# A decode step's attention and MLP in one kernel: the tile framework's scheduling against one section with semaphores of its own, with TensorE's products in hardware loops

## The chip, the cores and the metric

The kernel runs on one core of a Trainium2 chip. The metric is the device time of one launch in microseconds; a time of a kernel is the median of its runs. Durations inside a kernel come from one profiled execution.

## What is computed

One token x of 1024 values goes through a layer norm, and then through two branches whose results are added to it:

```python
xn = layernorm(x)
return x + A(xn, k_cache, v_cache, wq, wo) + B(xn, w1, w2, w3, w4)

# A: 32 query heads, 4 key/value heads, 65536 cached positions of 128 values
q = xn @ wq                                   # 1024 -> 32 x 128
p = softmax(q . k / sqrt(128))                # each of 4 caches serves 8 heads
A = (p @ v) @ wo                              # 4096 -> 1024

# B: two small networks, gelu in its tanh form
h  = gelu(layernorm(xn) @ w1)                 # 1024 -> 1024
hs = shifted(h) @ w2                          # with one token, all shifts give zero
x1 = xn + hs
B  = x1 + gelu(layernorm(x1) @ w3) @ w4       # 1024 -> 3584 -> 1024
```

All inputs are bf16. The two caches are 67 MB each, and everything that is read makes 170 MB.

## The kernel before

**Slots and items.** Three buffers in SBUF, `slot`, hold 128 partitions x 32768 bf16 (8.39 MB) each. The work is a list of items, and an item is what fills one slot: `wq`, `K(g,r)` and `V(g,r)` (g is one of four cache heads, r one of two halves of 32768 positions), `w3`, `w12` (w1 and w2), `w4`, and three items of `wo` (20 rows; 8; 3 and 1). Here a row of a weight means one of the blocks of 128 x 1024 that the view splits it into. The order is

wq, K(0,0), V(0,0), w3, w12, K(0,1), V(0,1), K(1,0), V(1,0), ... , K(3,1), w4, V(3,1), wo, wo, wo.

An item is computed when its turn in the list comes; ahead of that, the transfers are issued on SP's queue up to two items further on (line 119). A transfer into a slot waits until the item that held the slot before, three places back, has been computed. The tile framework puts the waits in from the tiles that each instruction reads and writes, and keeps each engine's instructions in the order of the program.

**K.** `compute_K` transposes a slot in place on VectorE in four pieces, `cg` (line 337, blocks of 32 x 32 of 4-byte pairs). After each piece TensorE makes 16 products of 128 x 512 (line 340) that add to four banks of PSUM, `sc`. After the fourth, VectorE takes the maximum (L344), two small transposes on TensorE (L346, L353) spread it as `nball`, ScalarE takes the exponential into `work` (L357), and VectorE transposes that (L359).

**V.** `compute_V` makes 64 products with 32 weight columns each into `oacc` (L393), where four column tiles of TensorE work side by side. For r = 0 the result is kept in `ob`; for r = 1 `group_weights` and `group_end` put both halves together and write the heads' output to `oT` (L408 to L423). So a K that follows a V with r = 1 comes on VectorE after that V's `group_end`.

**Rows.** `row_acc` (L161) multiplies one weight column (`oT`, `hT` or `gT`) with one row in four quarters of 256, each in a column tile of its own, and adds to `psB`:

```python
for j in range(4):
    nc.tensor.matmul(psB[32 * j:32 * j + 1, 0:NQ], lhsT=lhsT, rhs=w_row[:, NQ * j:NQ * (j + 1)], ...)
```

All 28 rows of w4, 8 of w2 and 32 of wo go through it, and so does x itself at the start (L201). `rows_product` (L242) makes the products with wq, w3 and w1. At the end VectorE copies `psB` (L435) and SP writes it out (L436).

Of the kernel before, what the change touches and what calls it, by code (L numbers as in the profile page):

```python
# [17 lines left out]
LOOKAHEAD = 2  # L18
WO_PIECES = (20, 8, 3, 1)
# [3 lines left out]
def kernel(  # L23
# [35 lines left out]
    NQ = NOUT // 4  # L59
    SCALE = float(DH) ** -0.5  # L60

    pad = ctx.enter_context(tc.tile_pool(name="pad", bufs=1))
    pad.tile([P, 96], F32, name="pad_t")
    big = ctx.enter_context(tc.tile_pool(name="big", bufs=SLOTS))
    const = ctx.enter_context(tc.tile_pool(name="const", bufs=1))
    small = ctx.enter_context(tc.tile_pool(name="small", bufs=2))
    ppool = ctx.enter_context(tc.tile_pool(name="pp", bufs=1))
    scr_pool = ctx.enter_context(tc.tile_pool(name="scr", bufs=1))
    ps_S = ctx.enter_context(tc.tile_pool(name="psS", bufs=1, space=bass.MemoryType.PSUM))
    ps_O = ctx.enter_context(tc.tile_pool(name="psO", bufs=1, space=bass.MemoryType.PSUM))  # L70
    ps_M = ctx.enter_context(tc.tile_pool(name="psM", bufs=2, space=bass.MemoryType.PSUM))
    ps_B = ctx.enter_context(tc.tile_pool(name="psB", bufs=1, space=bass.MemoryType.PSUM))
# [4 lines left out]
    wo_v = A_wo.rearrange("(m c) n -> m c n", c=OC)  # L77
# [5 lines left out]
    items = [("wq",), ("K", 0, 0), ("V", 0, 0), ("w3",), ("w12",)]  # L83
# [4 lines left out]
    items.insert(len(items) - 1, ("w4",))  # L88
    items += [("wo", 0), ("wo", 1), ("wo", 2)]

    st = {}

    def work():
        return ppool.tile([P, HF * 512], BF16, name="work")[:]

    def issue(item):
        kind = item[0]
        t = big.tile([P, KEYS], BF16, name="slot")
        if kind == "wq":
            loads = [(0, wq_v)]  # L100
        elif kind == "w3":
            loads = [(0, w3_v)]
        elif kind == "w4":
            loads = [(0, w4_v)]
        elif kind == "w12":
            loads = [(0, w1_v), (KEYS // 2, w2_v)]
        elif kind == "wo":
            pieces = [item[1]] if item[1] < 2 else list(range(2, len(WO_PIECES)))
            loads = []
            for q in pieces:  # L110
                c0 = wo_start[q]
                at = (c0 - wo_start[pieces[0]]) * NOUT
                loads.append((at, wo_v[:, c0:c0 + WO_PIECES[q], :].rearrange("p c n -> p (c n)")))
        else:
            cache = A_k_cache if kind == "K" else A_v_cache
            _, g, r = item
            loads = [(0, cache[0, g, r * KEYS:(r + 1) * KEYS, :].rearrange("(p k) d -> p (k d)", p=P))]
        for at, src in loads:
            nc.sync.dma_start(out=t[:, at:at + src.shape[-1]], in_=src)
        st[item] = t  # L120

    x_bf = const.tile([P, DC], BF16, name="x_bf")
    nc.scalar.dma_start(out=x_bf[:], in_=A_x[0, 0, :].rearrange("(p c) -> p c", c=DC))
    wk0 = work()
    qrow = wk0[:, 0:1024].rearrange("p (b n) -> p b n", b=2)
    psel = wk0[:, 1024:1536].rearrange("p (b m) -> p b m", b=4)
    x_q = wk0[:, 1536:1536 + NQ]
    ones_f = wk0[:, 1792:2048].bitcast(F32)
    nc.vector.memset(x_q, 0.0)
    nc.scalar.dma_start(out=x_q[0:P:32, :], in_=A_x[0, 0, :].rearrange("(j n) -> j n", j=4))  # L130

    n_issued = [0]

    def ensure(upto):
        while n_issued[0] <= min(upto, len(items) - 1):
            issue(items[n_issued[0]])
            n_issued[0] += 1

    ensure(LOOKAHEAD)

    ident_bf = const.tile([P, P], BF16, name="ident_bf")
    make_identity(nc, ident_bf[:])
    ident_f = const.tile([P, P], F32, name="ident_f")
    make_identity(nc, ident_f[:])
    eps_t = const.tile([P, 1], F32, name="eps_t")
    nc.gpsimd.memset(eps_t[:], LN_EPS)
    nc.gpsimd.memset(ones_f, 1.0)  # L147
    xpad = const.tile([P, DC, 32], BF16, name="xpad")
    nc.gpsimd.memset(xpad[:], 0.0)
    QS = P + 24  # L150
    qst = []
    for i in range(2):
        q_ = const.tile([P, 4, QS], BF16, name=f"qst{i}")
        nc.gpsimd.memset(q_[:], 0.0)
        qst.append(q_)

    psB = ps_B.tile([P, 512], F32, name="psB")

    def row_acc(lhsT, w_row):
        for j in range(4):  # L160
            nc.tensor.matmul(psB[32 * j:32 * j + 1, 0:NQ], lhsT=lhsT, rhs=w_row[:, NQ * j:NQ * (j + 1)],  # L161
                             start=False, stop=False, tile_position=(0, 32 * j),
                             skip_group_check=True)

    xT = const.tile([P, DC], F32, name="xT")
    nc.vector.tensor_copy(out=xT[:], in_=x_bf[:])  # L166

    def layernorm(src, tag):
        rowsum = const.tile([P, 1], F32, name=f"ln_rowsum_{tag}")
        nc.vector.reduce_sum(out=rowsum[:], in_=src[:], axis=AX.X)  # L170
        pm = ps_M.tile([P, 512], F32, name="pm_ln", tag="pm")
        nc.tensor.matmul(pm[:, 0:1], lhsT=ones_f, rhs=rowsum[:], start=True, stop=True)  # L172
        negmean = const.tile([P, 1], F32, name=f"ln_negmean_{tag}")
        nc.vector.tensor_scalar(out=negmean[:], in0=pm[:, 0:1], scalar1=-1.0 / D, scalar2=None, op0=ALU.mult)
        cen = const.tile([P, DC], F32, name=f"ln_cen_{tag}")
        nc.vector.tensor_scalar(out=cen[:], in0=src[:], scalar1=negmean[:, 0:1], scalar2=None, op0=ALU.add)
        sq = const.tile([P, DC], F32, name=f"ln_sq_{tag}")
        rowsq = const.tile([P, 1], F32, name=f"ln_rowsq_{tag}")
        nc.vector.tensor_tensor_reduce(out=sq[:], in0=cen[:], in1=cen[:], scale=1.0, scalar=0.0,
                                       op0=ALU.mult, op1=ALU.add, accum_out=rowsq[:])  # L180
        nc.tensor.matmul(pm[:, 1:2], lhsT=ones_f, rhs=rowsq[:], start=True, stop=True)
        std = const.tile([P, 1], F32, name=f"ln_std_{tag}")
        nc.scalar.activation(out=std[:], in_=pm[:, 1:2], func=ACTF.Sqrt, bias=eps_t[:, 0:1], scale=1.0 / D)
        rstd = const.tile([P, 1], F32, name=f"ln_rstd_{tag}")
        nc.vector.reciprocal(out=rstd[:], in_=std[:])
        normed = const.tile([P, DC], F32, name=f"ln_out_{tag}")
        nc.vector.tensor_scalar(out=normed[:], in0=cen[:], scalar1=rstd[:, 0:1], scalar2=None, op0=ALU.mult)
        return normed, negmean, rstd

    xn, negmean1, rstd1 = layernorm(xT, "a")  # L190
    nc.vector.tensor_copy(out=xpad[:, :, 0:1], in_=xn[:].unsqueeze(2))
    xn2, _, _ = layernorm(xn, "b")

    ln_s1 = const.tile([P, 1], F32, name="ln_s1")
    nc.vector.tensor_scalar(out=ln_s1[:], in0=rstd1[:], scalar1=1.0, scalar2=None, op0=ALU.add)
    ln_s2 = const.tile([P, 1], F32, name="ln_s2")
    nc.vector.tensor_tensor(out=ln_s2[:], in0=negmean1[:], in1=rstd1[:], op=ALU.mult)
    accx = wk0[:, 0:2 * NQ].bitcast(F32)
    nc.vector.tensor_scalar(out=accx, in0=x_q, scalar1=ln_s1[:, 0:1], scalar2=ln_s2[:, 0:1],
                            op0=ALU.mult, op1=ALU.add)  # L200
    nc.tensor.matmul(psB[:, 0:NQ], lhsT=ident_f[:], rhs=accx, start=True, stop=False, skip_group_check=True)  # L201

    sel32 = const.tile([P, 32], F32, name="sel32")
    nc.vector.tensor_tensor(out=sel32[:], in0=ident_f[:, 0:32], in1=ident_f[:, 32:64], op=ALU.add)
    nc.vector.tensor_tensor(out=sel32[:], in0=sel32[:], in1=ident_f[:, 64:96], op=ALU.add)
    nc.vector.tensor_tensor(out=sel32[:], in0=sel32[:], in1=ident_f[:, 96:128], op=ALU.add)
    mask16 = const.tile([P, 16], F32, name="mask16")
    nc.vector.tensor_tensor(out=mask16[:], in0=sel32[:, 0:16], in1=sel32[:, 16:32], op=ALU.add)
    mask64 = const.tile([P, 64], F32, name="mask64")
    nc.vector.tensor_tensor(out=mask64[:], in0=ident_f[:, 0:64], in1=ident_f[:, 64:128], op=ALU.add)  # L210
    dmask = const.tile([P, 4], F32, name="dmask")
    nc.vector.reduce_sum(out=dmask[:], in_=sel32[:].rearrange("p (cg h) -> p cg h", h=8), axis=AX.X)
    mask4 = const.tile([P, 4], F32, name="mask4")
# [114 lines left out]
    def compute_K(g, r):  # L328
# [34 lines left out]
        if r == NT - 1:  # L363
            group_weights(g)
# [108 lines left out]
```

## Time and profile before

| | us |
|---|---|
| median of 3 runs | 402.91 (402.84 to 402.95) |
| profiled execution, its time | 402.66 |
| profiled execution, its span | 400.9 |
| PE busy | 204.0 |
| VectorE (DVE) busy | 209.0 |
| ScalarE (ACT) busy | 27.3 |
| mean granted clock of TensorE | 0.796 |

The span goes from the first to the last instruction of the profiled execution, and its time is 1.76 us longer. In the rows of the profile, PE is TensorE, PEld its weight loads, SPq the queue in which SP issues transfers; "L340" is line 340 of the kernel. In a timeline, a row gives start, duration, engine, line, operation and count, and in brackets how long the engine sat idle before and what ended that. Before: 1,489 products and as many weight loads on TensorE, 40 transposes on VectorE.

### The profile page before, as it was taken

What the parts mean: (1) busy time and instruction counts of PE and PEld (TensorE: products, weight loads), DVE (VectorE), ACT (ScalarE), POOL (GpSimd) and SP (SyncE); (2) the same over time, 40 slices, a digit from 0 to 9 for tenths busy, and PEclk for the clock granted to TensorE, in tenths of its full rate; (3) what the DMA queues carried; (4) which work ended last, traced back from release to release, by engine and by line L of the source; (5) the groups of instructions that cost most, each with busy time, mean ns of one, the idle gap of its engine ahead of it and who ended that gap; (6) DMA issues with size and microseconds to landing.
All of it is one profiled execution on the core that took longest, in us unless ns stands there. A gap on an engine that the chain in (4) does not pass through costs nothing.

```text
span 400.9 us, 3366 instructions
## 1 busy us (share of the span) xinstructions
PE 204.0 (51%) x1489; PEld 85.4 (21%) x1489; DVE 209.0 (52%) x190; ACT 27.3 (7%) x33; POOL 5.9 (1%) x27
## 2 busy tenths in 40 slices
PE   0016393660079148741965295529453935496235
PEld 0003131220023013310322042204121412143113
DVE  0022992230196559634954894279358841885120
ACT  0002002110000300020002000100200020002000
POOL 1010000000000000000000000000000000000000
PEclk9999698695569587967895689679975976599588
DMA  9999999999999999999999999999999999999994
GB/s 406 425 425 419 419 420 452 401 489 419 425 433 419 419 484 427 419 432 438 420 419 471 432 420 438 438 420 438 451 419 425 433 445 436 419 455 419 414 416 174
DMA packets 3773, 170.07 MB, mean 424 GB/s; under 512 B 552, under 2 KB 560, under 8 KB 816
## 3 DMA queue, kind: packets, MB, share of 16 engines
q1 hardware_dynamic: 3608, 169.87, 98.1%
q8 instruction: 11, 0.18, 0.2%
q10 hardware_dynamic: 152, 0.00, 0.0%
q14 instruction: 2, 0.02, 0.0%
HBM read 169.87 MB, written 0.00 MB: 424 GB/s over the span
## 4 chain that ended last, share of the span: by engine, by line
DMA 48%; PE 26%; DVE 20%; ACT 4%; issue 1%; ACTq 0%; SPq 0%; POOL 0%; DVEq 0%
DMA slot<-in_A_k_cache_dram 28%; PE sc L340 14%; DVE slot L337 12%; DMA slot<-in_A_v_cache_dram 10%; PE oacc L393 8%; DMA work<-in_A_x_dram 7%; DMA slot<-in_A_wo_dram 3%; DVE work L359 3%; DVE mx L344 3%; ACT work L357 3%; PE rows L242 1%; ACT L357 1%; PE pm_mx L346 0%; DVE m L348 0%; DVE og L408 0%
## 5 line engine op out<-in xcount | busy, mean ns | idle before, releaser
L340 PE MATMUL sc<-slot,qst 128*128 128x512 bf16 x512 | 129.8, 415 | 75.6 <-DVE slot L337 75.6
L337 DVE STREAM_TRANSPOSE slot<-slot 128x4096 f32<-128x4096 f32 x32 | 139.4, 4413 | 49.4 <-DMA slot<-in_A_k_cache_dram 49.3
L340 PEld LDWEIGHTS <-qst 128*128 128x128 bf16 x512 | 52.1, 103 | 152.1 <-DVE slot L337 55.9
L393 PE MATMUL oacc<-slot,work 128*32 128x512 bf16 x512 | 43.3, 513 | 45.3 <-DVE work L359 35.7
L344 DVE TENSOR_REDUCE mx<-sc 128x1 f32<-128x2048 f32 x8 | 18.3, 2292 | 30.2 <-PE sc L340 30.2
L393 PEld LDWEIGHTS <-work 128*32 128x32 bf16 x512 | 16.3, 124 | 69.2 <-DVE work L359 36.3
L357 ACT ACTIVATE work<-sc,nball 128x2048 bf16<-128x2048 f32 x8 | 15.7, 1967 | 193.5 <-DVE nball L355 193.5
L359 DVE STREAM_TRANSPOSE work<-work 128x2048 bf16<-128x2048 bf16 x8 | 18.5, 2311 | 19.1 <-ACT work L357 19.1
L408 DVE SCALAR_TENSOR_TENSOR og<-oacc,wm,og 128x128 f32<-128x128 f32 x16 | 5.6, 351 | 22.2 <-PE oacc L393 21.8
L172 PE MATMUL pm_ln<-ln_rowsum_a,work 128*128 128x1 f32 x2 | 0.6, 362 | 27.7 <-POOL work L147 27.7
L166 DVE CAST xT<-x_bf 128x8 f32<-128x8 bf16 x1 | 0.2, 172 | 22.0 <-DMA x_bf<-in_A_x_dram 22.0
L346 PE MATMUL pm_mx<-ident_f,mx 128*1 128x128 f32 x8 | 2.3, 283 | 18.1 <-DVE mx L344 18.1
L242 PE MATMUL rows<-slot,xpad 128*32 128x512 bf16 (+1 forms) x144 | 9.6, 397 | 0.9 <-DMA slot<-in_B_w_dram 0.9
L161 PE MATMUL psB<-slot,oT 128*1 128x256 bf16 x128 | 6.3, 362 | 6.3 <-DMA slot<-in_A_wo_dram 6.1
L357 ACT ACT_TABLE_LOAD x2 | 2.6, 1283 | 73.5 <-DVE nball L355 73.5
L287 DVE TENSOR_TENSOR work<-pm_h,mask 128x448 f32<-128x448 f32 x1 | 0.6, 625 | 11.4 <-PE pm_h L284 11.4
L172 PEld LDWEIGHTS pm_ln<-ln_rowsum_a,work 128*128 128x128 f32 x2 | 0.5, 310 | 27.6 <-POOL work L147 27.6
L435 DVE CAST work<-psB 97x256 bf16<-97x256 f32 x1 | 0.4, 425 | 11.4 <-PE psB L161 11.4
L161 PEld LDWEIGHTS <-oT 128*1 128x1 bf16 x128 | 3.9, 108 | 8.8 <-issue 5.6
L242 PEld LDWEIGHTS <-xpad 128*32 128x32 bf16 x144 | 4.4, 103 | 5.7 <-DMA slot<-in_B_w_dram 1.8
L346 PEld LDWEIGHTS pm_mx<-ident_f,mx 128*1 128x1 f32 x8 | 0.6, 79 | 21.9 <-DVE mx L344 21.9
L412 PE MATMUL pm_e<-og,sel8x 128*32 128x129 f32 x8 | 1.6, 282 | 6.6 <-DVE og L408 6.6
(102 smaller groups left out, 65.4 us busy)
## 6 DMA issues: line engine op xcount, KB each, us to landing
slot<-in_B_w_dram SPq DMA_DIRECT2D x2, 7168.0 KB, 37.7
slot<-in_A_wo_dram SPq DMA_DIRECT2D x1, 5120.0 KB, 27.0
slot<-in_B_w_dram SPq DMA_DIRECT2D x2, 2048.0 KB, 23.1
slot<-in_A_wo_dram SPq DMA_DIRECT2D x1, 2048.0 KB, 26.3
slot<-in_A_wo_dram SPq DMA_DIRECT2D x1, 768.0 KB, 13.5
slot<-in_A_wo_dram SPq DMA_DIRECT2D x1, 256.0 KB
slot<-in_A_k_cache_dram SPq DMA_DIRECT2D x8, 41.7
slot<-in_A_v_cache_dram SPq DMA_DIRECT2D x8, 38.6
```

The source lines that it names most:

```text
L161: nc.tensor.matmul(psB[32 * j:32 * j + 1, 0:NQ], lhsT=lhsT, rhs=w_row[:, NQ * j:NQ * (j + 1)], start=False, stop=False, tile_position=(0, ...
L172: nc.tensor.matmul(pm[:, 0:1], lhsT=ones_f, rhs=rowsum[:], start=True, stop=True)
L242: nc.tensor.matmul(acc[32 * j:32 * j + 32, bk, 0:width], lhsT=xp[:, c, :], rhs=wt[:, c, ch * width:(ch + 1) * width], start=(c == 0), stop ...
L337: nc.vector.transpose(out=kf[:, cg, :], in_=kf[:, cg, :])
L340: nc.tensor.matmul(sc[:, hf, :], lhsT=qst[g % 2][:, bp, 24 - 8 * cg:24 - 8 * cg + P], rhs=kr[:, cg, hf, :, bp // 2, :, bp % 2], start=(cg ...
L344: nc.vector.reduce_max(out=mx[:], in_=sc[:].rearrange("p h n -> p (h n)"), axis=AX.X)
L346: nc.tensor.transpose(pm[0:1, 0:P], mx[:, 0:1], ident_f[:])
L357: nc.scalar.activation(out=pT, in_=sc[:], func=ACTF.Exp, bias=nball[:, r:r + 1], scale=SCALE, accum_out=lall[:, r:r + 1])
L359: nc.vector.transpose(out=pT, in_=pT)
L393: nc.tensor.matmul(oacc[32 * u:32 * (u + 1), :], lhsT=pT[:, hf, 32 * t:32 * (t + 1)], rhs=vt[:, :, hf, t, :], start=(hf == 0 and t < 4), s ...
L408: nc.vector.scalar_tensor_tensor(out=og[:, 0:P], in0=oacc[:, P * cg:P * (cg + 1)], scalar=wm[:, 1, cg:cg + 1], in1=og[:, 0:P], op0=ALU.mul ...
L412: nc.tensor.matmul(pe[rows, 0:P + 1], lhsT=sel8x[:], rhs=og[:], start=True, stop=True, tile_position=(0, 32 * g))
```

## The change

The kernel is written anew as one critical section of the tile framework, in which the framework puts in no waits. A class, `Flow`, keeps one semaphore for each engine and one for each slot's transfers, notes for each named piece of data who wrote and who read it last, and puts in the waits. Every engine keeps the order of the program, as before.

- K's products: instead of 16 products after each of four transposes, 32 after each two (`CGS = 2`), in a hardware loop of four turns over the banks of `sc`.
- 14 rows of w4 with w1 (item `wa`), the other 14 with w2 (item `wb`), and the first ten rows of wo go through `rows_loop`: a hardware loop of 2 or 5 rows a turn, each row two products of 1 x 512 into `psR`, without column tiles. x is added to `psR` too, early.
- The other 22 rows of wo go through `row_acc` as before, into a bank of `sc`; after the second ten, `psR` is copied to `work` by VectorE and ScalarE and added by four more products ("fold").
- The items: `wa` comes behind V(0,1), `wb` has w4's former place in front of V(3,1), the first item of wo is loaded as 10 and 10 rows.
- Tiles of their own for some scratch data (`ones_f` lies in `og` rather than in `work`), one PSUM bank `pm` for all small products rather than two in turn; the rest of the arithmetic is the same.

```diff
-WO_PIECES = (20, 8, 3, 1)
+WO_PIECES = (10, 10, 8, 3, 1)
+WO_ITEMS = ((0, 1), (2,), (3, 4))
+WO_UNROLL = 5
+CGS = 2
...
+    def op(self, eng, reads, writes, emit, times=1):
+
+        self._wait(eng, reads, writes)
+        sem = self.sem(eng)
...
+        emit(signal)
+        self.counts[eng] += times
+        self._note((eng, self.counts[eng]), reads, writes)
...
-    items = [("wq",), ("K", 0, 0), ("V", 0, 0), ("w3",), ("w12",)]
+    items = [("wq",), ("K", 0, 0), ("V", 0, 0), ("w3",)]
     for g in range(HKV):
         for r in range(NT):
             if (g, r) != (0, 0):
                 items += [("K", g, r), ("V", g, r)]
-    items.insert(len(items) - 1, ("w4",))
+            if (g, r) == (0, 1):
+                items += [("wa",)]
+    items.insert(len(items) - 1, ("wb",))
     items += [("wo", 0), ("wo", 1), ("wo", 2)]
...
+    section = ExitStack()
+    section.enter_context(tc.tile_critical())
+    fl = Flow(nc, ctx)
...
+    def rows_loop(lhsT, wt, n, reads, unroll):
+
+        lv = lhsT.rearrange("p (c u) -> p c u", u=unroll)
+        wv = wt.rearrange("p (c u h n) -> p c u h n", u=unroll, h=2, n=NH)
+
+        def emit(signal):
+            with nc.tensor.Fori(0, n // unroll) as c:
+                for u in range(unroll):
+                    for h in range(2):
+                        ins = nc.tensor.matmul(psR[0:1, h, :], lhsT=lv[:, bass.ds(c, 1), u],
+                                               rhs=wv[:, bass.ds(c, 1), u, h, :],
+                                               start=False, stop=False, skip_group_check=True)
+                signal(ins)
+        op("T", reads, ["psR"], emit, times=n // unroll)
...
+    def compute_wb(s):
+        slot = slots[s]
+        rows_loop(hT[:, FH:FC], slot[:, 0:FH * NOUT], FC - FH, ["hT", ("slot", s)], unroll=2)
+        rows_loop(gT[:], slot[:, KEYS // 2:KEYS // 2 + DC * D], DC, ["gT", ("slot", s, 1)], unroll=2)
...
         for cg in range(4):
-            nc.vector.transpose(out=kf[:, cg, :], in_=kf[:, cg, :])
-            for bp in range(4):
-                for hf in range(HF):
-                    nc.tensor.matmul(sc[:, hf, :], lhsT=qst[g % 2][:, bp, 24 - 8 * cg:24 - 8 * cg + P],
-                                     rhs=kr[:, cg, hf, :, bp // 2, :, bp % 2],
-                                     start=(cg == 0 and bp == 0), stop=(cg == 3 and bp == 3))
...
+        for cp in range(4 // CGS):
+            for cg in range(CGS * cp, CGS * cp + CGS):
+                v([("slot", s)], [("kt", s, cg)], lambda e: e.transpose(out=kf[:, cg, :], in_=kf[:, cg, :]))
+
+            def emit(signal):
+                with nc.tensor.Fori(0, HF) as hf:
+                    for cg in range(CGS * cp, CGS * cp + CGS):
+                        for bp in range(4):
+                            ins = nc.tensor.matmul(sc[:, bass.ds(hf, 1), :],
+                                                   lhsT=qst[g % 2][:, bp, 24 - 8 * cg:24 - 8 * cg + P],
+                                                   rhs=kr[:, cg, bass.ds(hf, 1), :, bp // 2, :, bp % 2],
+                                                   start=(cg == 0 and bp == 0), stop=(cg == 3 and bp == 3),
+                                                   skip_group_check=True)
+                    signal(ins)
+            op("T", [("kt", s, cg) for cg in range(CGS * cp, CGS * cp + CGS)] + [("qst", g % 2)], ["sc"], emit, times=HF)
...
+            if q == 0:
+                rows_loop(oT[:, c0:c0 + WO_PIECES[q]], w, WO_PIECES[q], ["oT", key], unroll=WO_UNROLL)
+                v(["psR"], ["fold0"] + WORK, lambda e: e.tensor_copy(out=fold[:, 0:NH], in_=psR[0:1, 0, :]))
+                one("S", ["psR"], ["fold1"], lambda e: e.copy(out=fold[:, NH:NOUT], in_=psR[0:1, 1, :]))
+                continue
...
+            op("T", ["oT", key], ["sc"], emit)
+            if q == 1:
+                op("T", ["fold0", "fold1", "ident_f"], ["sc"], lambda signal: signal(row_acc(ident_f[0:1, 0:1], fold)))
```

## The prediction

> **What bounds the kernel now.** I read the page first: the slices and the queues.
>
> ```profile
> span 400.9 us, 3366 instructions
> ...
> DMA  9999999999999999999999999999999999999994
> ...
> q1 hardware_dynamic: 3608, 169.87, 98.1%
> q8 instruction: 11, 0.18, 0.2%
> ```
>
> The transfer engines are full in 39 of 40 slices and only the last is thin: the bytes set the time, and no byte of the inputs is saved by the change. What can move is the start, the end, the 0.2% of queue 8 (TensorE's own program, fetched in 11 packets), or a stage of computing that becomes so long that the queue waits for it. So the next view is the timeline of one group, K(1,1) and V(1,1), which tells how far computing is from being the bound.
>
> ```profile
> 185.99 17.42 DVE L337 STREAM_TRANSPOSE slot<-slot 128x4096 f32<-128x4096 f32 x4 [9.36 <-DMA slot<-in_A_k_cache_dram]
> 190.49 8.42 PE L340 MATMUL sc<-slot,qst 128*128 128x512 bf16 x32 [8.80 <-DVE slot L337]
> 199.14 3.64 PE L340 MATMUL sc<-slot,qst 128*128 128x512 bf16 x16 [0.23 <-DVE slot L337]
> 203.47 3.64 PE L340 MATMUL sc<-slot,qst 128*128 128x512 bf16 x16 [0.69 <-DVE slot L337]
> ...
> 207.15 2.29 DVE L344 TENSOR_REDUCE mx<-sc 128x1 f32<-128x2048 f32 x1 [3.73 <-PE sc L340]
> ...
> 215.33 6.15 PE L393 MATMUL oacc<-slot,work 128*32 128x512 bf16 x64 [4.69 <-DVE work L359]
> ...
> 224.72 17.42 DVE L337 STREAM_TRANSPOSE slot<-slot 128x4096 f32<-128x4096 f32 x4
> ```
>
> Columns: start, duration, engine, what, and in brackets the idle time before and who ended it. VectorE's program is serial: an odd K (r=1), its softmax, its V, then the next K. From 185.99 to 224.72 that is 38.73 us; an even K needs no V on VectorE and takes 29.3 us (224.72 to the end of its L359 at 254.01). Two K and two V are 4 x 8.39 MB, which at the page's 433 GB/s of a full slice land in 77.5 us; computing takes 68.0. The slack is 9.5 us for each group of heads, and it shows as the idle of 9.36 before the first row and as no idle before the last.
>
> The third view is the timeline of the end.
>
> ```profile
> 366.50 2.02 PE L161 MATMUL psB<-slot,hT 128*1 128x256 bf16 x67
> ...
> 378.08 5.00 PE L393 MATMUL oacc<-slot,work 128*32 128x512 bf16 x64 [9.55 <-DMA slot<-in_A_v_cache_dram]
> ...
> 386.15 0.18 DVE L423 CAST oT<-o 32x32 bf16<-32x32 f32 x1
> ...
> 390.12 4.44 PE L161 MATMUL psB<-slot,oT 128*1 128x256 bf16 x80 [5.01 <-DMA slot<-in_A_wo_dram]
> ...
> 394.90 1.04 PE L161 MATMUL psB<-slot,oT 128*1 128x256 bf16 x32 [0.35 <-DMA slot<-in_A_wo_dram]
> ...
> 396.71 0.93 PE L161 MATMUL psB<-slot,oT 128*1 128x256 bf16 x16 [0.76 <-DMA slot<-in_A_wo_dram]
> ...
> 397.69 0.42 DVE L435 CAST work<-psB 97x256 bf16<-97x256 f32 x1 [11.36 <-PE psB L161]
> ```
>
> Each step of TensorE waits for a landing here, the last for the last piece of wo at about 397.3. After it come 0.3 us of products, the cast, and 2.8 us to the span's end; the time is 1.76 us longer than the span (402.66 to 400.9). I sum against 402.66; the median of the runs is 402.91, so 0.25 is added at the end. A difference of 0.2%, 0.8 us, is about what a measurement of this kernel can tell from none.
>
> **K's products in two loops.** Before, 16 products follow each of the four transposes (4.36 us each), and after the last one 3.64 us are left. Now the first loop waits for two transposes, the second for all four, so 32 products are left. Their pace at full clock is 3.64/16 = 228 ns, 7.3 us a loop. The first loop starts cold: the windows of L340 for a K that starts at 306.8 give
>
> ```profile
> 306.50:311.00 4.50, 4.24 (x11) 1.46 (x12) 0.50 0.97 422
> ...
> 315.50:320.00 4.50, 4.50 (x22) 2.00 (x21) 1.00 1.04 451
> ```
>
> (products, then weight loads, clock): 11 in 4.24 us at clock 0.50, 385 ns each. K(1,1) lost 8.42 - 7.3 = 1.1 us to it, this one up to 2.5 (6.1 us cold x 0.41); I take 1.8. The first loop then runs from 8.7 to 17.8 us after the landing, past the transposes' 17.4, and the second ends at 25.1 where it was 21.1: +4.0 us a K, between 3.65 (no overlap lost) and 4.7. Two a group are 8.0 of the 9.5 us of slack, so in the middle of the kernel DMA still sets the pace, with 1.5 us in hand. Below 3.65 the cost can't go: 32 products must stream after the last transpose.
>
> No row shows a loop, its register instructions or its branch. The built program has, for each product of the loop, one register instruction beside weights and product, and an add and a branch for each eight. Low bound: 16 ns an instruction, from 64 of TensorE's in 1.04 us (L161 x32 with its loads); all hidden under 228 ns. High bound: SP's DMA issue of 0.33 us, the nearest instruction that a sequencer works out itself; then a product takes 0.35 or more. Since these run on TensorE's own queue, I take the low end for the products, with 0.2 us for entering a loop and 0.1 for each turn that isn't hidden (both estimates between those rows). [...]
>
> **w4 and w2 rows in loops.** Before, w4's 112 quarter-row products run four column tiles side by side: 1.03 + 0.61 + 2.02 = 3.7 us, finished before V(3,1) lands. Now 22 rows (14 of w4, 8 of w2) are 44 products of 512 columns with one weight column each: 44 x 0.228 = 10.0 us, 11 turns 1.1, two entries 0.4, 11.5 us. They stand on TensorE between K(3,1)'s second small transpose and V(3,1). That transpose ended at 366.6 and now 370.6; so V(3,1), which landed at 378.05, starts at 382.1, four late. If the clock drops in the 3.5 us before them, as it did within 2 to 5 us of the ends of other K's, add up to 2.5. [...] V's 64 products took 5.00 with 3 us of them cold at 16 per us; warm, at 23 per us, 2.8. So V ends at 384.9 (383.1 before), oT follows 3.25 later: 388.2.
>
> **wo.** Before, 20 rows landed together at 390.1. Now the first ten have landed by about 384, and ten rows in a loop are 20 x 0.228 + 0.4 = 5.0 us: 393.2. Ten more rows unrolled, 40 x 32.5 ns = 1.3 (the two copies of the fold, 0.42 each by the cast's row, run beside them): 394.5. The fold's four float32 products: the nearest row is L201's two in 1.06, I take 0.8: 395.3. Then 32 products, landed at 394.9, 1.04: 396.3; the last two pieces land at 396.7 and 397.3 as before. All warm, the end is where it was, with 1 us in hand. Against that stand: a cold start of w4's rows (0 to 2.5), of wo's loop (0 to 3.1, 20 x 0.157), turns of 0.2 rather than 0.1 (1.3), and a late K(3,1) (0 to 1). I take 3.2 of these 8 us, less the 1 in hand: +2.2.
>
> **Smaller edits.** One section: all engines wait once more at its start and end; the row is the 0.7 us that SP waits for TensorE's sequencer at L457. I take 0.4 (0 to 1.0). TensorE's program goes from 192,256 to 141,632 bytes as built, 11.7 to 8.6 packets of queue 8's size. A packet took 0.002 x 400.9 x 16 / 11 = 1.2 us of one engine of 16, and a transfer ends with its slowest engine: between 0 and -1.2, I take -0.2, since eight are left. ones_f in a tile of its own no longer waits for the second read of x (27.39 to 23.0): hidden, K(0,0) lands at about 42. w1 and w2 apart, a third table load for gelu and one more for exp, 1.28 us each, in front of K(1,0)'s landing: hidden by its 9 us. Of the moved transfers, w1 with half of w4 now comes behind V(0,1) and the rest ahead of V(3,1); SP issues each when the slot three items back is free, and the tightest is wo's second item: its slot is freed by w4's rows at 382.1, while wo's first is in flight until 390. So one transfer stays queued throughout.
>
> Sum: 402.66 + 2.2 + 0.4 - 0.2 + 0.25 = 405.3 us.
>
> **Rivals.** (B) The end stays on the landings: clock warm, turns hidden. 402.66 + 0.4 - 0.2 + 0.25, about 403.1. For it: the sum above needs cold clocks to lose. (C) The loops are bound by their sequencer. A group has 128 products, so its 1.5 us are gone at 240 ns a product; at 260 ns a group is 128 x 0.032 = 4.1 us longer, 2.6 past the slack, in three groups 7.8, with 2 more for 64 row products: 415; at 300 ns about 433. For it: register operands in every product; against: 16 ns an instruction. (D) Faster: the fetches that go were those of the slowest engine, up to 1.2 us, with B's end and no cost of the section: 401.7. Against: eight remain, on one engine in two. [...]
>
> **How the numbers follow.** Forecast (0.8 to 8 us slower) 0.44, B 0.19, C 0.20, D 0.12, E 0.05. Slower: all of the forecast, C and E, 0.69, less a little for hidden ends: 0.67; same: B and that, 0.20; faster: D and the low edge of B, 0.13. The range leaves out D's low part and the upper half of C: 401.9 to 419.
>
> **What would show it.** After: first K loop ending near 17.8 us after the landing and the second near 25; w4's and w2's loops between 370.6 and 382 and V(3,1) waiting for them, not for its landing; queue 8 with eight packets. Wrong, if products in the loop start more than 240 ns apart at clock 1.00 (then C), if slices before the last show less than 9 for DMA, or if V(3,1) still waits for DMA (then B or D).

## The result, and the profile after

The changed kernel takes 407.38 us (405.54 to 408.11, five runs) against 402.90 (402.83 to 402.95) for the kernel before: 4.5 us slower, a ratio of 1.0100 with a 95% interval of 1.0073 to 1.0127. The profiled execution took 407.46, its span 405.4. The page of the changed kernel, with the same parts as shown of the kernel before:

```profile
span 405.4 us, 4094 instructions
...
DMA  9999999999999999999999999999999999999990
...
q1 hardware_dynamic: 3896, 169.87, 97.2%
q8 instruction: 8, 0.13, 0.1%
...
DMA 46%; PE 33%; DVE 15%; issue 3%; ACT 1%; SPq 0%; POOL 0%; ACTq 0%
```

The same bytes move, and the queues are full until the last slice, which is empty now: the landings are over at least 7 us before the end (the inputs' last bytes move before 398). In the chain of waits (last line) TensorE has 33% where it had 26% (page of before: DMA 48%; PE 26%). The middle of the kernel still keeps pace with the transfers; the loss is at the end. The timeline of TensorE and VectorE from K(3,1) on:

```profile
344.45 17.43 DVE L447 STREAM_TRANSPOSE slot<-slot 128x4096 f32<-128x4096 f32 x4 [2.42 <-DMA slot<-in_A_k_cache_dram]
353.58 16.42 PE L453 MATMUL sc<-slot,qst 128*128 x64 [6.53 <-DVE slot L447]
373.69 8.74 PE L338 MATMUL psR<-slot,hT 128*1 x28
382.27 3.19 PE L338 MATMUL psR<-slot,gT 128*1 x14
...
385.52 3.82 PE L501 MATMUL oacc<-slot,work 128*32 128x512 bf16 x58
392.41 0.18 DVE L525 CAST oT<-o 32x32 bf16<-32x32 f32 x1
392.95 5.50 PE L338 MATMUL psR<-slot,oT 128*1 x18 [1.58 <-DVE oT L525]
...
399.91 0.61 PE L532 MATMUL sc<-work,ident_f 1*1 1x256 f32 x8
400.44 1.48 PE L532 MATMUL sc<-slot,oT 128*1 128x256 bf16 x48
401.98 0.42 DVE L559 CAST ob<-sc 97x256 bf16<-97x256 f32 x1 [2.38 <-PE sc L532]
```

After K(3,1) has landed, no bracket names a DMA any more. V(3,1) (L501) starts the moment the rows end: its first six products, from 385.08 on, stand among the last two of the rows. The last 48 products, for which the kernel before waited piece by piece, run as one block. The end is one chain of TensorE.

### The profile page after: what moved, and what is told of

It reads as the page before. It is cut to its first block, busy times and chain, and to the rows that moved or that the text cites. A ratio compares the mean times of both kernels' runs of the same rounds, so it can differ in the third digit from the quotient of the medians.

```text
span 405.4 us, 4094 instructions
## 1 busy us (share of the span) xinstructions
PE 221.9 (55%) x1407; PEld 91.8 (23%) x1407; DVE 210.5 (52%) x191; ACT 30.9 (8%) x36; POOL 6.3 (2%) x28
## 4 chain that ended last, share of the span: by engine, by line
DMA 46%; PE 33%; DVE 15%; issue 3%; ACT 1%; SPq 0%; POOL 0%; ACTq 0%
DMA slot<-in_A_k_cache_dram 46%; PE sc L453 20%; DVE slot L447 11%; PE psR L338 6%; PE oacc L501 5%; DVE sm L460 2%; PE sc L532 1%; DVE og L513 1%; DVE work L471 1%; ACT work L469 1%; PE sc L322 0%; ACT L469 0%; PE pm L461 0%; DVE sm L462 0%; PE pm L466 0%
## 5 line engine op out<-in xcount | busy, mean ns | idle before, releaser
L453 PE MATMUL sc<-slot,qst 128*128 x512 | 128.3, 413 | 84.1 <-DVE slot L447 83.9
L453 PEld LDWEIGHTS sc<-slot,qst 128*128 128x128 bf16 x512 | 52.4, 102 | 159.9 <-issue 109.6
L501 PE MATMUL oacc<-slot,work 128*32 128x512 bf16 x512 | 44.2, 515 | 37.5 <-DVE work L471 21.9
L460 DVE TENSOR_REDUCE sm<-sc 128x1 f32<-128x2048 f32 x8 | 18.3, 2291 | 62.5 <-PE sc L453 62.5
L501 PEld LDWEIGHTS oacc<-slot,work 128*32 128x32 bf16 x512 | 18.5, 124 | 59.7 <-issue 55.1
L469 ACT ACTIVATE work<-sc,sm 128x2048 bf16<-128x2048 f32 x8 | 15.7, 1967 | 151.3 <-DVE sm L467 151.3
L513 DVE SCALAR_TENSOR_TENSOR og<-oacc,sm,og 128x128 f32<-128x128 f32 x16 | 5.6, 350 | 20.8 <-PE oacc L501 20.4
L338 PE MATMUL psR<-slot,hT 128*1 x56 | 15.9, 433 | 0.3
L322 PE MATMUL sc<-slot,xpad 128*32 128x512 bf16 (+1 forms) x144 | 11.0, 437 | 4.3 <-DMA slot<-in_A_wq_dram 4.3
L322 PEld LDWEIGHTS sc<-slot,xpad 128*32 128x32 bf16 x144 | 5.4, 111 | 8.9 <-DMA slot<-in_A_wq_dram 4.4
L338 PE MATMUL psR<-slot,oT 128*1 x20 | 5.9, 465 | 1.6 <-DVE oT L525 1.6
```

The costliest lines, as they stand in the source:

```text
L322: ins = nc.tensor.matmul(sc[32 * j:32 * j + 32, bk, 0:width], lhsT=xpad[:, c, :], rhs=wt[:, c, ch * width:(ch + 1) * width], start=(c == 0 ...
L338: ins = nc.tensor.matmul(psR[0:1, h, :], lhsT=lv[:, bass.ds(c, 1), u], rhs=wv[:, bass.ds(c, 1), u, h, :], start=False, stop=False, skip_gr ...
L453: ins = nc.tensor.matmul(sc[:, bass.ds(hf, 1), :], lhsT=qst[g % 2][:, bp, 24 - 8 * cg:24 - 8 * cg + P], rhs=kr[:, cg, bass.ds(hf, 1), :, b ...
L460: v(["sc"], ["mx"], lambda e: e.reduce_max(out=mx, in_=sc[:].rearrange("p h n -> p (h n)"), axis=AX.X))
L469: one("S", ["sc", ("nball", r)], WORK + [("lall", r)], lambda e: e.activation(out=pT, in_=sc[:], func=ACTF.Exp, bias=nball[:, r:r + 1], sc ...
L501: ins = nc.tensor.matmul(oacc[32 * u:32 * (u + 1), :], lhsT=pT[:, hf, 32 * t:32 * (t + 1)], rhs=vt[:, :, hf, t, :], start=(hf == 0 and t < 4),
```

## The experiments

**1. Which half of the change costs it.** Four kernels, each the changed one with one part undone. Ratios are to the kernel before, and `...` marks what is left out of an edit.

The items put together as before (w1 with w2, though still behind V(0,1), and w4 whole in front of V(3,1)); loops and widths stay:

```diff
-            loads = [(0, w1_v), (KEYS // 2, w4_v[:, 0:FH * NOUT])]
+            loads = [(0, w1_v), (KEYS // 2, w2_v)]
-            loads = [(0, w4_v[:, FH * NOUT:FC * NOUT]), (KEYS // 2, w2_v)]
+            loads = [(0, w4_v)]
...
```

> Undoes the halves of w4 alone: w1 with w2 behind V(0,1), the whole of w4 (28 rows in the loop) in front of V(3,1). Theory 1 (the end is a chain on TensorE: K(3,1)'s landing, 32 products after the last transpose, row loops, V(3,1), wo's loop): K(3,1) lands 2.5 us earlier (342 for 344.4), but 12 products more stand in front of V(3,1), 2.7 us at 223 ns; so the time stays within 1 us of 407.4. Theory 2 (late landing of K(3,1) alone makes the loss): 2.5 us less, about 404.9. Theory 3 (turns and entries of loops cost): 3 turns more and 2.5 us earlier, about 405.5.

Measured: 407.32 (406.41 to 407.87), ratio 1.0102 (1.0085 to 1.0119), the same as the changed kernel. In its trace K(3,1)'s transposes start at 343.10 instead of 344.45, and the rows are longer:

```profile
371.61 14.51 PE L338 MATMUL psR<-slot,hT 128*1 x56
```

56 products in 14.51 us instead of 44 in 12.0, from an earlier start, so V(3,1) begins at 385.86, 0.8 us after the 385.08 of the changed kernel. The halves move two terms of opposite sign and come out at nothing in the time. Of the 2.5 us that were expected at the landing 1.35 came.

K's products in sixteens after each transpose, in the same hardware loop:

```diff
-CGS = 2
+CGS = 1
```

> CGS = 1: a loop of 16 products after each transpose, still four turns, so eight more loops... four loops a K rather than two. Theory 1: after the last transpose 16 products are left rather than 32, K ends 3.6 us earlier and the rest of the end moves with it: 403.6 to 404. Theory 3 (entries and turns of loops cost): twice as many entries and turns of half the work; each K would end no more than 2 us earlier, and the time would be 405 or more.

Measured: 402.66 (402.50 to 404.32), ratio 0.9999 (0.9990 to 1.0009): the whole loss is gone, with the rows still in loops and still 512 wide, and the time is 0.9 us below the range of theory 1. Its timeline:

```profile
344.48 17.42 DVE L447 STREAM_TRANSPOSE slot<-slot 128x4096 f32<-128x4096 f32 x4 [8.32 <-DMA slot<-in_A_k_cache_dram]
...
362.27 4.10 PE L453 MATMUL sc<-slot,qst 128*128 x16 [0.23 <-issue]
...
381.12 3.67 PE L501 MATMUL oacc<-slot,work 128*32 128x512 bf16 x64
388.39 4.04 PE L338 MATMUL psR<-slot,oT 128*1 x18 [1.58 <-DVE oT L525]
394.43 1.04 PE L532 MATMUL sc<-slot,oT 128*1 128x256 bf16 x32
396.01 0.92 PE L532 MATMUL sc<-slot,oT 128*1 128x256 bf16 x16 [0.53 <-DMA slot<-in_A_wo_dram]
```

K(3,1) lands at the same time as in the changed kernel (344.48), and its products end 21.9 us after that instead of 25.6: 3.7 us. The last cast comes 5.0 us earlier (396.98 against 401.98), because V(3,1) and wo's loop were also faster, by 0.6 and 1.5 us. The loop ran at clock 1.00 here and at 0.76 in the changed kernel; why is not shown, and theory 1 had not counted on it. Waits for the last landings take 1.0 us of this back: the last 16 products wait for DMA again, by 0.53 us. The bracket before the transposes, 8.32 us against 2.42, shows that the slack of the middle is back too.

All rows in four column tiles of 256 ("tiled" from here on), written out, in a bank of their own, with no fold; halves and K's loops of 32 stay:

```diff
-                        ins = nc.tensor.matmul(psR[0:1, h, :], lhsT=lv[:, bass.ds(c, 1), u],
-                                               rhs=wv[:, bass.ds(c, 1), u, h, :], ...)
+                    ins = nc.tensor.matmul(psB[32 * j:32 * j + 1, 0:NQ], lhsT=lhsT[:, c:c + 1],
+                                           rhs=wt[:, c * NOUT + NQ * j:c * NOUT + NQ * (j + 1)],
+                                           ..., tile_position=(0, 32 * j), ...)
...
```

> All rows of w4, w2 and wo unrolled on four column tiles of 256 as before, into one PSUM bank of their own, no fold; K's loops and the halves stay. Theory 1: 88 quarter products take some 3 us in place of 12, V(3,1) starts at its landing or its weights (378.4), oT is there at 386.7, wo follows its landings: 402.9 to 403.6. Theory 2 (the later landing of K(3,1) and its longer tail hold V(3,1)): V(3,1) starts at 380 or later and the time stays at 405 or more.

Measured: 403.66 (403.35 to 403.81), ratio 1.0018 (1.0009 to 1.0028), 0.1 us over the upper end of theory 1 and 1.3 below theory 2. The timeline:

```profile
372.84 2.42 PE L333 MATMUL psR<-slot,hT 128*1 128x256 bf16 x56
375.03 1.94 PE L333 MATMUL psR<-slot,gT 128*1 128x256 bf16 x32
377.69 3.64 PE L507 MATMUL oacc<-slot,work 128*32 128x512 bf16 x64 [0.73 <-DMA slot<-in_A_v_cache_dram]
```

The same 22 rows take 4.1 us instead of 12.0, V(3,1) waits for its own landing (377.69) and not for rows, and 3.7 us come back although K's last loop still ends 24.9 us after the landing. So the loss has two halves on one chain, and either of them alone is all but hidden.

K's products written out, in the same order of 32 after two transposes:

```diff
-                with nc.tensor.Fori(0, HF) as hf:
+                for hf in range(HF):
...
```

> K's products unrolled, same order, still 32 after the second and the fourth transpose; only the loops are gone. Theory 1: a product in the loop already takes 223 ns, so nothing but the entry of 0.35 us goes: within 0.5 us of 407.4, with more packets on queue 8. Theory 3 (register work and turns): 64 products a K get faster, 1 to 3 us less.

Measured: 406.43 (406.09 to 407.86), ratio 1.0097 (1.0076 to 1.0118). That is 0.95 us less, between the two theories, and the single runs of both kernels overlap. In the profiled execution the second 32 products end 25.1 us after the landing instead of 25.6. The loop as such is worth a microsecond at most; the waiting for two transposes is what costs.

**2. Loops or widths.** The rows of the loops written out, one weight column and 512 columns a product as in the change:

```diff
-            with nc.tensor.Fori(0, n // unroll) as c:
+            for c in range(n // unroll):
...
```

> The rows of w1's companion w4, w2 and the first ten of wo are written out instead of looped; still one weight column and 512 columns a product, no column tiles; items, K's loops, fold as in the changed kernel. Theory 1 (the width of the products costs, the loop form does not): w4's and w2's late rows take 11.5 to 12 us as in the changed kernel (12.0), wo's first ten rows 5.5 (5.50 there); time 406.4 to 407.5. Theory 2 (the loop form costs, by register instructions and branches between products): the 44 late products fall towards the 44 x 0.223 us that L453's best loop shows, 9.8 us, wo's to 4.5, and the time by some 3 us to 404.5. Theory 3 (a longer program costs more fetches): over 408.

Measured: 407.62 (405.82 to 408.13), ratio 1.0108 (1.0091 to 1.0125), 0.1 us above the upper end of theory 1 and 3 us away from theory 2. The late rows took 11.2 us (12.0 in the loop), and the tiled ones 4.1. The width is the price: 44 products with one weight column and 512 output columns, without column tiles, took 11.2 us written out and 12.0 in the loop; the same rows as 88 products of 256 in four column tiles took 4.1. Two equal stretches still show what a turn of the loop costs. The first half of w4's rows early in the kernel, first in the kernel with these rows written out, then in the changed kernel:

```profile
145.26 6.21 PE L338 MATMUL psR<-slot,hT 128*1 128x512 bf16 x28
```

```profile
145.96 7.44 PE L338 MATMUL psR<-slot,hT 128*1 x28
```

Seven turns with four products each take 1.2 us more, 0.17 a turn. The clock in the changed kernel was 1.00 from 145 to 152 us; in the other one the page's slice from 141 to 151 us shows 0.9 or more.

**3. What is left when both halves are undone.** The single gains are 4.7 and 3.7 us, and only 4.5 lie between the kernels. Three kernels go back further: the section with none of the halves, loops and widths ("the section alone"; the place of w1 and w2 behind V(0,1), wo's first item in two transfers, and the scratch tiles stay as changed); the same with K's loops of 16; and the changed kernel with K's products in sixteens ("16s"), tiled rows and the halves of w4 kept. Their edits are those above put together.

> One section with semaphores, and the rest as in the kernel before: K's products in sixteens after each transpose and written out, all rows of w4, w2 and wo in four column tiles, w1 with w2 and w4 whole. Theory 1 (the section costs 0 to 0.4 us at its start and the end stays on the landings): 402.5 to 403.3, four products of the last rows within 0.5 us of where they stood. Rival (the section itself costs more, by later DMA issues or because the framework's order was better): 404 or more. Rival (the earlier x and the separate scratch tiles are worth something): below 402.2.

> As the section alone, but K's products in a hardware loop of four turns with four products each (16 after each transpose). Theory 1 (the loop is hidden behind the next transpose): same as the section alone within 0.3 us, 402.5 to 403.3; the last 16 products of K(3,1) take 4.1 us with the loop and 3.7 without, which the wait for V(3,1)'s landing hides. Rival (the loop's entry adds to every K's path): 0.4 us for each of eight K, but only as far as no landing hides it: up to 1 us.

> The changed kernel with both of the costly parts undone: K's products in loops of 16 after each transpose, and all rows in four column tiles; the halves of w4 are kept. Singly they gave 4.7 and 3.7 us, 8.4 together, but only 4.5 lie between the two kernels. Theory 1 (the landings of wo bound the end once TensorE has any slack): 402.4 to 403.2, no faster than with the 16s alone. Rival (the gains add): 399 to 401.

Measured: 403.71 (ratio 1.0025, 1.0015 to 1.0035), 403.88 (1.0022, 1.0013 to 1.0032) and 404.08 (1.0030, 1.0018 to 1.0042). The gains do not add. The loop in sixteens changes nothing against the written-out form, as expected. But all three missed: they are 0.8 to 1.2 us over the kernel before, and with tiled rows 1.4 us over the same kernel with looped rows, which theory 1 had as equal. The last products of the section alone:

```profile
395.37 2.84 PE L537 MATMUL psR<-slot,oT 128*1 128x256 bf16 x48 [2.77 <-DMA slot<-in_A_wo_dram]
```

Its last 48 products take 59 ns each where the 16s with looped rows needed 32.5 (1.04 us for 32). The windows give the clock (a row ends with clock, DMA share and GB/s), first of the section alone, then of the 16s with looped rows:

```profile
394.00:398.00 4.00, 2.63 (x48) 0.50 0.42 170
```

```profile
394.00:398.00 4.00, 2.25 (x56) 1.00 0.32 127
```

So there are two candidates: a low clock, or late transfers. In the section alone I filled TensorE's idle time at the end with 30 products that nobody reads:

```diff
+    def filler(n):
+        ...
+                ins = nc.tensor.matmul(psR[:, 1, :], lhsT=ident_bf[:], rhs=qst[0][...][:, 0:512], start=True, stop=True, ...)
```

> The section alone, with 30 products more of 128 x 512 into an unused bank of PSUM (their result is not read): 6 behind V(3,1), 6 behind the heads' sums, 4 behind wo's first ten rows and 14 behind the second ten, so that TensorE works on while it waits for wo's landings. Theory (the section alone lost its 0.8 us mostly because its last 48 products ran at a granted clock of 0.50, at 59 ns each, where the kernel before and the 16s with looped rows ran at 1.00): the clock stays at 1.00 from 390 us on, the last 48 take 1.5 to 2.1 us instead of 2.84, and the time falls by 0.5 to 1.3 us, to 402.4 to 403.2. Rival (the last pieces of wo land late in this kernel, whatever the clock): the clock rises, the products shorten, and the time stays at 403.4 to 403.8 with the idle time before the last products grown.

Measured: 403.64, ratio 1.0018 (1.0009 to 1.0027); no gain.

```profile
395.93 1.04 PE L541 MATMUL psR<-slot,oT 128*1 128x256 bf16 x32 [0.47 <-DMA slot<-in_A_wo_dram]
397.73 0.20 PEld L541 LDWEIGHTS psR<-slot,oT 128*1 128x1 bf16 x12 [1.06 <-DMA slot<-in_A_wo_dram]
398.35 0.09 PEld L541 LDWEIGHTS psR<-slot,oT 128*1 128x1 bf16 x4 [0.42 <-DMA slot<-in_A_wo_dram]
```

The clock is at 1.00, 32 products take 1.04 us, and the wait grows instead: the weight loads for the last two pieces start at 397.73 and 398.35, where they started at 396.0 and 396.6 with the 16s and looped rows. The rival holds: the landings are late. Next I asked whether the early issue of wo's second item makes them late. Two kernels with 16s, tiled rows, halves and the filler, without and with

```diff
-        if i + SLOTS < len(items):
+        if i + SLOTS < len(items) and items[i + SLOTS] != ("wo", 1):
+            if items[i + SLOTS] == ("wo", 2):
+                fl._wait("Q", ["oacc"], [])
+                load(i + SLOTS - 1)
```

> The kernel with K in sixteens, rows in column tiles and halves of w4 (404.08 before), with the 30 products more that keep TensorE busy at the end as in the section with warm clock. Here only the last landings are asked for, with the clock at 1.00. wo's second item is still issued as soon as w2's and w4's rows have freed its slot, near 374. If the early issue spreads the landings: last weight loads for wo at or after 397, time 403.3 to 404.0, same as the section alone with warm clock (403.64). If the landings depend on something else (clock, rows in loops): they stand where they stood with 16s and looped rows, 396.0 and 396.6, and the time is 402.5 to 403.0.

> The same with one change: the second item of wo is issued only once V(3,1)'s products are done, near 382, as late as in the 16s with looped rows (381), where the first 20 rows then had the queues to themselves. If the early issue is what made the last landings late: second ten rows land before 389, the last pieces at 396.0 to 396.6, time 402.4 to 403.0, about 1 us under its partner. If it is not: same as its partner within 0.4 us.

Measured: 403.68 (1.0022, 1.0013 to 1.0031) and 403.54 (1.0019, 1.0009 to 1.0028); the last piece but one is there at 397.35 and 397.43. The order of issue is not it. Among what is left of the difference (the PSUM bank of the rows and the transfer of the x that is added differ too) is the length of the program: 9 to 12 packets of queue 8 in the tiled kernels, 8 with 16s and looped rows. The last kernel is the one with the 16s and looped rows, with 192 small products written out where TensorE is idle before K(3,1):

```diff
+                for _ in range(192):
+                    ins = nc.tensor.matmul(pm[0:1, 0:16], lhsT=ident_bf[:, 0:1], rhs=ident_bf[:, 0:16], ...)
+            op("T", ["ident_bf"], ["pm"], emit0)
```

> The changed kernel with K in sixteens (402.66, queue 8 with eight packets, one of them after 365 us), with 192 products more of one weight column and 16 columns, written out, on TensorE between V(3,0) and K(3,1), where it sits idle for 6.5 us; their result is not read. They make TensorE's program longer by one or two packets of queue 8, and nothing else. If a fetch costs the end what it takes of one transfer engine (rival D's premise, up to 1.2 us a packet): the last weight loads for wo move from 396.0 and 396.6 to 396.7 to 398, as where the rows are in column tiles (397.4 and 398.0 with ten packets), and the time is 403.2 to 404.0. If not: 402.5 to 402.9, and the 1 us between looped rows and column tiles stays open.

Measured: 403.62 (402.98 to 404.95), ratio 1.0016 (1.0007 to 1.0025): 1.0 us slower than without them, inside the range of the first theory.

```profile
342.92 4.95 PE L448 MATMUL pm<-ident_bf 128*1 128x16 bf16 x192
...
349.97 8.48 PE L460 MATMUL sc<-slot,qst 128*128 x32 [2.10 <-DVE slot L454]
...
390.26 5.68 PE L338 MATMUL psR<-slot,oT 128*1 x18 [1.57 <-DVE oT L532]
```

The products sit in idle time: K's wait for the transpose has 2.10 us to spare. Queue 8 has ten packets, two more, and the time is 1 us longer. That the fetches do it is not shown. K(3,1) lands at 345.17, 0.7 us later, but 0.3 of that stands already at V(3,0)'s products (336.64 against 336.31), ahead of the added ones, and up to 300 us queue 8 had moved five packets in both kernels. This profiled execution was also the slowest of its eleven and bound by TensorE at the end: wo's loop took 5.68 us at a clock of 0.57 (390 to 394), where it took 4.04 at 1.00 without the 192 products. So the clock is a rival that this run leaves open. And 9 packets in the other kernels cost as much as 12. No kernel here beat the one before by more than a measurement can tell; the 16s with looped rows equal it.

## Why the prediction came out as it did

**The case.** The likeliest case happened: the end is a chain of TensorE, the middle keeps pace. The forecast was 405.3, the result 407.38, inside the range of 401.9 to 419. The chain was forecast to cost 2.4 us over 402.91 and cost 4.5, so its size was short by 2.1 us.

**K's tail: right.** The second loop ends 25.6 us after the landing (353.58 + 16.42 against 344.45), where 25.1 was said; 0.4 of that is that the first loop starts 9.1 instead of 8.7 after it. The 16s take 3.7 of it back. The slack of the middle was all but used up, as computed: two of the later K (233.27 and 308.94) start with no wait, two with 0.85 and 2.42 us.

**K(3,1)'s landing: the step that failed.** I kept it where the kernel before had it, and gave "a late K(3,1)" 0 to 1 us:

```profile
341.97 17.42 DVE L337 STREAM_TRANSPOSE slot<-slot 128x4096 f32<-128x4096 f32 x4 [10.05 <-DMA slot<-in_A_k_cache_dram]
```

It came at 344.45, +2.5. The change's own list of items says why: ahead of K(3,1) half of w4 (3.67 MB) goes where w2 (2.1 MB) went. 1.57 MB at the 433 GB/s of a full slice (page of before) are 3.6 us of the queue, of which 2.5 show; where the other 1.1 went is open. With the old items and the old order of K (the section alone) it landed at 341.91, counted back from K's first product (346.41) by the 4.50 us between the two in the kernel before. The five kernels with the halves of which a row shows it have it between 344.45 and 345.17, with K in 32s and in 16s; the kernel before has 341.97, and the one with the old items 343.10. I had followed where the transfers are issued, and not what stood in the queue in front of them.

**Rows: right.** 373.69 to 385.7 is 12.0 us (the last product starts at 385.51, and I add the 0.2 us after which the next one could start), said 11.5. The cold start that I gave up to 2.5 us is there, but short:

```profile
374.00:378.00 4.00, 4.00 (x11) 0.50 0.89 381
...
382.00:386.00 4.00, 4.00 (x36) 1.00 1.04 442
```

(products, clock, DMA share, GB/s.) 11 products in the first 4 us at 0.50, and full speed in the row 8 us later, in which V(3,1)'s products begin too. With K's products written out, the same gap stood in front of the same rows, but the first 28 products took 7.32 us instead of 8.74, about the 7.44 of the 28 early ones at clock 1.00, and all of them 11.3 us (373.25 to 384.58, counted the same way). So whether the rows start cold is not settled by the gap alone, and here it cost about 0.7 us.

**V(3,1): mis-sized.** I took 2.8 us warm, from a pace of 23 products per us. It takes 3.64 to 3.71 in the experiments (3.67 in the kernel with 16s, at clock 1.00), and 4.3 from its first product here (385.08 to 389.34). Its first six products stand among the last rows, so that 0.8 us more than said are left.

**wo's loop: mis-sized.** Said 5.0, measured 5.75 (392.95 to 398.70, its last start at 398.50 and 0.2) at a clock of 0.76 between 394 and 398, and it started 0.35 after `oT`. In the kernel with 16s, at 1.00, 18 of its 20 products took 4.04 instead of 5.50. The ten rows and the fold behind it took 1.74 us, 0.4 less than said; of that the fold's products took 0.6 where I had 0.8.

**The sum.** Step by step the chain is late by 3.1 us at the first row (2.5 landing, 0.6 K's end and the small products behind it), 3.6 at the last, 4.4 at V's end, 5.5 behind wo's loop, 5.1 in front of the last block. As worked out, that block would have ended at 396.8, had it waited for nothing, 0.8 ahead of the 397.6 of the kernel before: so products end 4.3 later, at 401.9. I had taken 3.2 of 8 us for all this, less 1 in hand, and in these 3.2 a late K(3,1), one of the 8, had a share of 0.4. It took 2.5, and the 2.1 between are what was missing. That the rest came out as allowed is in part luck: the clock at wo's loop, 0.76 here, stood at 1.00 in the kernel with 16s.

**Rivals.** B and D are out for this kernel: its end does not wait for landings. C is out by the pace of the loop. The second loop of K(3,0):

```profile
326.73 7.13 PE L453 MATMUL sc<-slot,qst 128*128 x32 [0.19 <-issue]
```

223 ns a product, no slower than the 228 written out. E, a loop for which parts of the program are fetched again at each turn, is out: queue 8 moved eight packets in all (0.13 MB, page of the changed kernel), no more than the 8.6 that I worked out from the program's size.

The turns are between: with eight products a turn they are hidden, with four they are not. K's sixteen products take 4.10 us in the loop and 3.65 written out, 0.11 us a turn, and the rows' 28 gave 0.17. The 0.1 us that I took for a turn was an estimate; it agrees with the first and not with the second.

**Section and fetch: not told apart.** I took +0.4 and -0.2. The section alone, with the changes that stay in it, costs 0.8 with 11 packets as before. Of it 0.2 come after the last transfer is issued (2.98 us to the end of the span where it was 2.76), and 0.6 stand at the last cast (398.26 against 397.69). The 16s with looped rows and eight packets are 1.0 under it (402.66 against 403.71), but no run shows that the fetches make this difference, so neither term is confirmed. In the changed kernel all but the 0.2 are hidden under TensorE's chain.

## What to carry to other kernels

Here the queue was full in 39 of 40 slices, and the cost of the change, 4.5 us, lay at the end: for such a kernel, write out the chain after the last large landing, product by product, and count which bytes stand in the queue ahead of it. Grouping work to save waits moved work behind the last wait: K's products ended 25.6 us after the landing in 32s and 21.9 in 16s. A hardware loop cost nothing visible with eight products of 512 columns a turn (223 ns a product, 228 written out), and 0.11 to 0.17 us a turn with four. But 22 rows through one column tile of four took 12.0 us against 4.1 through all four, loop or not. Two costs lay on one chain, and undoing one of them gave 4.7 or 3.7 us of the 4.5: of two such costs one has to be undone, not both.

## What was not expected

- Moving w4's first half early made the late rows 2.9 us shorter and K(3,1)'s landing 1.35 us later. V(3,1) began only 0.8 us earlier, and the two halves of one edit measured zero in the time.
- 192 small products in idle time cost 1.0 us of a kernel that waits for transfers, and the section alone 0.8 us, with products as in the kernel before. The cause is open: clock (403.64 at 1.00, 403.71 at 0.50) and order of issue (403.68 and 403.54) are ruled out for the tiled kernels, the program's fetches are not, and for the 192 products the clock is not either.
- x lands at 13.4 us instead of 23.0, though its transfer is issued at 0.92 us and was issued at 0.74; why is not shown. wq's products start at 23.0 instead of 34.4, when wq has landed, and nothing gains: K(0,0) starts at 42.3 as before.
